# The root of the mean square by token: partition sums by ones and ScalarE's Sqrt in place of roots on diagonals

## The chip, the core and the metric

The kernel runs on one core of one Trainium2 chip. A core has TensorE (PE, matmuls; PEld is its loading of weights), VectorE (DVE), ScalarE (ACT), GpSimd (POOL) and the queue that issues DMAs (SP). The engines run beside one another and wait for each other by semaphores; each takes its own instructions in the order in which the program has them. PE writes its results into PSUM, from where DVE and ACT read them in this kernel. The metric is the device time of one execution in microseconds.

## The reference, cut to what matters

Eight sequences of 576 tokens go through windowed attention with 8 heads (four with a plain window of 32, four with a window of 128 of which every fourth token counts), then through a gated feed-forward layer whose input is normalised by token:

```python
scores = np.where(masks, scale * q @ k.T, -1e9)
attn = softmax(scores)
x = (attn @ v)                       # (4608 tokens, 512)
rms = np.sqrt(np.mean(x * x, axis=-1, keepdims=True) + 1e-06)
xn = x / rms * rms_g
g = xn @ w_gate                      # (512, 1536)
silu = g * (1.0 / (1.0 + np.exp(-g)))
val = xn @ w_val
return (silu * val @ w_out)          # (1536, 512)
```

The change is about the line with `rms`.

## The kernel before

The 4608 tokens are cut into 16 units of 288 (`U`). The activations lie with the 512 features on partitions, as four chunks of 128 (`c`), and the tokens along the free axis. A unit's feed-forward layer runs over 12 pieces `j` of 128 hidden features. For each j there are three steps: `gate` (12 matmuls for g), `val` (12 for v) and `proj` of the piece before (12 into the four accumulators `acc`), so 36 steps for a unit. From unit 1 on every operand is split into two float32r parts, a high one (a cast) and a low one (the difference), and a product takes three matmuls: high by high, high by low, low by high. Unit 0 works with whole float32 operands while the weights are still being loaded and decoded; unit 1 runs while they are being split.

The code writes the order out by hand. `now` counts steps; `later(dt, rank, fn)` puts work for the other engines into the step `now + dt`, and `flush`, ahead of each step's matmuls, issues what was put there, by rank. So a step's matmuls and what the other engines do with the results of the step before stand side by side. `plan` lays the attention of unit u (scores, transposes, outputs) over the 36 steps in which unit u-1 is multiplied; its dictionary `events` also holds two entries for the mean square of unit u:

- `"sum"` (L749) calls `rms_sum`, and `"apply"` (L750) calls `rms_apply`. For units from 2 on they come 3 and 5 steps behind the last attention output: in the step of v for j=9 and in that of g for j=10.

Where the mean square comes from: `square` (L423) squares each chunk of x on ACT and adds the four into one tile `xsq` (128 partitions by 288 tokens); the last addition is on DVE (L433). What is missing then is the sum over the 128 partitions and the root. Before the change:

- `rms_sum` (L526) has PE multiply `xsq`, in three blocks of 96 tokens, with a column of 1/512 (`inv`); the result `rps` has tokens on partitions, 96 by 3.
- `rms_root` (L534) adds 1e-6 on DVE (L536), raises to the power -0.5 on POOL (L537), and splits the result into two float32r parts on POOL (L542, L543).
- `spread`, a step later, lays both parts on diagonals: the high one by one DVE multiplication with the identity (L551), the low one by three ACT instructions (L555).
- `rms_apply` (L567) has PE multiply ones with the two diagonals, so that each of the 128 partitions holds the inverse root for all 288 tokens (`bps`, in PSUM). `normal(c)` (L585, DVE) multiplies a chunk by it and by the gain; `part(c)` splits it (L602 on ACT, L603 on DVE or POOL).

Around it each j has, outside PE: `tanh` of g on ACT (L661), one step behind the gate; `silu` on DVE (L666); `prod` with v on DVE (L679); the split of the result on ACT (L690) and POOL (L691), which `proj` needs two steps later. g and v have two PSUM banks that change places (`bank`): g of j+1 is written where v of j was, and v of j+1 where g of j was. The probabilities transposed by PE in a step go into the tail of such a bank, in a proj step into that of g of the same j (tile `t`). `split` casts keys and queries of the next unit (L330, L339 on ACT; L335 on POOL, L344 on DVE), and the softmax of the next unit takes L361 to L366 on DVE, L376 on ACT, L385 to L386 on DVE and L391 on POOL.

Unit 0 has its own way (`spread_first`, whole float32 tiles).

Of the kernel before, what the change touches and what calls it, by code (L numbers as in the profile page):

```python
# [9 lines left out]
F32 = mybir.dt.float32  # L10
# [10 lines left out]
P = 128  # L21
# [4 lines left out]
QB = 96  # L26
# [41 lines left out]
def attn_moe(ctx: ExitStack, tc: tile.TileContext, qk_in, v_in, w_gate, w_val, w_out, rms_g, outT):  # L68
# [14 lines left out]
    G.memset(one, 1.0)  # L83
    ones = cst.tile([P, P], F32R, name="ones")
    A.copy(out=ones, in_=one.to_broadcast([P, P]))
    inv = cst.tile([P, 2], F32, name="inv")
    G.memset(inv, 1.0 / DM)
    mhalf = cst.tile([QB, U // QB], F32, name="mhalf")
# [21 lines left out]
    def later(dt, rank, fn):  # L110
        put_off.setdefault(now[0] + dt, []).append((rank, fn))
# [411 lines left out]
    NB = U // QB  # L523
    rst = {}

    def rms_sum(u):  # L526
        r_ps = ps.tile([QB, NB, 2], F32, tag="o", name=f"rps_{u}")
        for i in range(NB):
            PE.matmul(r_ps[:, i, :], xsq[u][:, i * QB:(i + 1) * QB], inv, start=True, stop=True)
        later(1, 0.1, lambda: rms_root(u, r_ps))  # L530
        if u == 0:
            later(1, 6, spread_first)

    def rms_root(u, r_ps):  # L534
        r = sb.tile([QB, NB], F32, tag="rst", name=f"rst_{u}", bufs=2)
        V.tensor_scalar(out=r, in0=r_ps[:, :, 0], scalar1=1e-6, scalar2=None, op0=ALU.add)  # L536
        G.tensor_tensor(out=r, in0=r, in1=mhalf, op=ALU.pow)  # L537
        if u == 0:
            rst[u] = [r]
            return  # L540
        r_hi, r_lo = (sb.tile([QB, NB], F32R, tag=f"rst_{p}", name=f"rst_{p}_{u}", bufs=1) for p in ("hi", "lo"))
        G.tensor_copy(out=r_hi, in_=r)  # L542
        G.tensor_tensor(out=r_lo, in0=r, in1=r_hi, op=ALU.subtract)  # L543
        rst[u] = []

        def spread():
            for p in (r_hi, r_lo):
                d = sb.tile([QB, NB, QB], F32R, tag="tmp", name=f"rd_{u}_{len(rst[u])}", bufs=2)
                rst[u].append(d)
                if p is r_hi:  # L550
                    V.tensor_tensor(out=d, in0=ident[:QB, None, :QB].to_broadcast([QB, NB, QB]),  # L551
                                    in1=p[:, :, None].bitcast(F32).to_broadcast([QB, NB, QB]), op=ALU.mult)
                    continue
                for i in range(NB):
                    A.activation(out=d[:, i, :], in_=ident, func=AF.Copy, scale=p[:, i:i + 1].bitcast(F32))  # L555
        later(1, 0.1, spread)

    def spread_first():
        r, = rst[0]
# [7 lines left out]
    def rms_apply(u):  # L567
        ds = rst.pop(u)
        b_ps = ps.tile([P, U], F32, tag="o", name=f"bps_{u}")
        for k, d in enumerate(ds):  # L570
            PE.matmul(b_ps, (ones if u else ones32)[:QB, :], d.rearrange("p i q -> p (i q)"),
                      start=k == 0, stop=k == len(ds) - 1)
        xs[u] = {}
        if u == 0:
            root.append(sb.tile([P, U], F32, tag="tmp", name="root", bufs=2))
            later(1, 0.62, lambda: V.tensor_copy(out=root[0], in_=b_ps))

        def normal(c):
            x = xraw[u, c]
            if u == 0:  # L580
                xn = sb.tile([P, U], F32, tag="xhi", name=f"xn_{c}", bufs=4)
                V.tensor_tensor(out=xn, in0=x, in1=b_ps, op=ALU.mult)
                xs[u][c] = xn
                return
            V.scalar_tensor_tensor(out=x, in0=x, scalar=gs[:, c:c + 1], in1=b_ps,  # L585
                                   op0=ALU.mult, op1=ALU.mult)

        def part(c):
            x = xraw.pop((u, c))
            k = (u * NC + c) % 6  # L590
            if u > 1 and not spare:
                spare.append(cst.tile([P, 3, U], F32R, tag=f"slot{state['free']}", name="spare"))
            if k == 5 and u > 1:
                hi = spare[0][:, 2]
            else:
                pool, tag, bufs = (sb, "xhi", 4) if k < 4 else (late[0], ("xhi", "ot")[k - 4], 1)
                hi = pool.tile([P, U], F32R, tag=tag, name=f"xhi_{u}_{c}", bufs=bufs)
            if c < 2 and u % 2 == 0:
                lo = spare[0][:, c]
            else:  # L600
                lo = late[0].tile([P, U], F32R, tag=f"xlo{c // 2}", name=f"xlo_{u}_{c}", bufs=2)
            A.copy(out=hi, in_=x)  # L602
            (V if c % 2 else G).tensor_tensor(out=lo, in0=x, in1=hi, op=ALU.subtract)  # L603
            xs[u][c] = (hi, lo)

        for c in range(NC):
            later((1, 2, 2, 3)[c] if u else 1, 0.6 + (0.03 * (c > 1) if u == 0 else 0), lambda c=c: normal(c))
            if u:
                later((2, 3, 4, 5)[c], 0.6, lambda c=c: part(c))


    hs, acc, gv = {}, {}, {}
# [132 lines left out]
    def plan(u, base, q_at, t_at, o_at):  # L745
        for b, *ts in zip(bursts(u), q_at, t_at, o_at):
            for kind, t in zip("qto", ts):
                events.setdefault(base + t, {})[kind] = b
        events.setdefault(base + o_at[-1] + (4 if u == 1 else 3), {})["sum"] = u  # L749
        events.setdefault(base + o_at[-1] + (4, 7, 5)[min(u, 2)], {})["apply"] = u  # L750

    def attend(t_ps, **tags):
        e = events.pop(now[0], {})
# [132 lines left out]
```

## Time and profile before

| | |
|---|---|
| median of 3 runs | 1148.58 us (1146.93 to 1150.12) |
| the profiled execution | 1148.22 us |
| its span, from first to last instruction | 1146.4 us |
| granted TensorE clock, mean | 0.997 |
| read from HBM, written | 71.08 MB, 9.44 MB |

The span is what the profile covers; the 1.8 us between it and the execution's time lie around it. The profile names an instruction by its line in the kernel, its engine, and output and input. A timeline has the start in microseconds from the beginning of the span, the length, and in square brackets the idle time of the engine just before it with what ended it. Matmuls are pipelined: one that is said to last 0.29 us begins 0.13 us behind the one before it. In a view of groups the columns behind the count are the busy time in all, the mean of one in ns, and the idle time ahead of them. Short pieces of a timeline may overlap by some 0.1 us on one engine, since the next instruction starts before the last one is through.

### The profile page before, as it was taken

To read this page: it belongs to the slowest core of one execution; us is meant where nothing else is said; L and a number is where in the kernel's file an instruction comes from. 1 tells how busy PE (TensorE), PEld (TensorE's weight loads), DVE (VectorE), ACT (ScalarE), POOL (GpSimd) and SP (SyncE) were. 2 spreads that over 40 slices of the span, in tenths; PEclk is the share of its full clock that TensorE was granted. 3 is DMA by queue.
4 is the path that set the end of the run, shared out by engine and by line. 5 is a ranking of instruction groups with operands and counts; after the bars stand their busy time and mean duration, and the time that the engine had idled before them with its cause. 6 is when DMAs were issued, how large, how long until landed. Compare 5 with 4: busy or idle time off the path is not lost.

```text
span 1146.4 us, 25956 instructions
## 1 busy us (share of the span) xinstructions
PE 1120.8 (98%) x8357; PEld 1088.0 (95%) x8357; DVE 793.4 (69%) x2893; ACT 714.6 (62%) x2610; POOL 620.8 (54%) x1073
## 2 busy tenths in 40 slices
PE   8898888999999999999999999999999999999998
PEld 7676778999999999999999999999999999999998
DVE  7889865867767586776758677585866758586411
ACT  5686676766657576675757657576765757576311
POOL 8235576655546465564547556465655646565211
PEclk9999999999999999999999999999999999999999
DMA  9555211311212121121212213121221312120000
GB/s 246 168 202 205 89 48 38 93 50 50 83 38 82 40 84 52 52 89 33 79 41 83 58 41 94 34 86 41 71 63 45 95 27 87 41 79 15 2 21 21
DMA packets 61545, 82.19 MB, mean 72 GB/s; under 512 B 7298, under 2 KB 41090, under 8 KB 61410
## 3 DMA queue, kind: packets, MB, share of 16 engines
q1 hardware_dynamic: 61410, 80.54, 23.6%
q8 instruction: 67, 1.10, 0.4%
q14 instruction: 68, 0.56, 0.2%
HBM read 71.08 MB, written 9.44 MB: 70 GB/s over the span
## 4 chain that ended last, share of the span: by engine, by line
PE 85%; DVE 6%; ACT 4%; issue 2%; DMA 1%; POOL 1%; POOLq 0%; SPq 0%; DVEq 0%; ACTq 0%
PE acc L622 8%; PE g L622 8%; PE v L622 8%; PE acc L623 8%; PE g L624 8%; PE g L623 8%; PE acc L624 8%; PE v L623 8%; PE v L624 8%; PE s L489 3%; PE o L477 3%; PE o L478 1%; PE busy L739 1%; ACT t L376 1%; DVE lo L243 1%
## 5 line engine op out<-in xcount | busy, mean ns | idle before, releaser
L691 POOL TENSOR_TENSOR hlo<-th,hhi 128x288 fp32r<-128x288 f32 x180 | 145.2, 807 | 201.5 <-ACT hhi L690 153.7
L624 PE MATMUL acc<-hhi,lo 128*128 128x288 f32 x720 | 212.2, 295 | 0.0
L391 POOL TENSOR_SCALAR t<-t,sum 72x72 f32<-72x72 f32 (+3 forms) x414 | 154.0, 384 | 71.9 <-DVE sum L386 65.2
L624 PE MATMUL v<-xhi,lo 128*128 128x288 f32 x612 | 180.8, 295 | 0.0
L624 PE MATMUL g<-xhi,lo 128*128 128x288 f32 x612 | 180.6, 295 | 0.0
L376 ACT ACTIVATE t<-t,sum 96x128 f32<-96x128 f32 (+3 forms) x448 | 165.6, 375 | 11.7 <-DVE sum L366 11.0
L690 ACT CAST hhi<-th 128x288 fp32r<-128x288 f32 x180 | 78.1, 434 | 141.0 <-DVE th L679 138.8
L305 POOL TENSOR_TENSOR vlo<-vt,vhi 128x128 fp32r<-128x128 f32 x196 | 93.3, 476 | 109.3 <-ACT vhi L301 96.9
L421 DVE TENSOR_TENSOR xraw<-o,xraw 64x96 f32<-64x96 f32 (+1 forms) x392 | 106.8, 272 | 56.4 <-ACT xraw L411 50.4
L661 ACT ACTIVATE th<-g 128x288 f32<-128x288 f32 x180 | 73.9, 410 | 106.6 <-PE g L624 87.7
L624 PEld LDWEIGHTS acc<-hhi,lo 128*128 128x128 f32 x720 | 135.6, 188 | 0.0
L666 DVE SCALAR_TENSOR_TENSOR th<-th,g 128x288 f32<-128x288 f32 x180 | 80.4, 447 | 69.4 <-ACT th L661 69.4
L624 PEld LDWEIGHTS v<-xhi,lo 128*128 128x128 f32 x612 | 115.3, 188 | 0.0
L624 PEld LDWEIGHTS g<-xhi,lo 128*128 128x128 f32 x612 | 115.0, 188 | 0.0
L622 PE MATMUL g<-xhi,hi_g 128*128 128x288 f32 x357 | 110.7, 310 | 1.6 <-DVE sum L385 0.9
L335 POOL TENSOR_TENSOR ks<-qk,ks 128x288 fp32r<-128x288 f32 (+2 forms) x112 | 111.0, 1005 | 0.0
L622 PE MATMUL acc<-hhi,hi_o 128*128 128x288 f32 x360 | 110.8, 308 | 0.0
L411 ACT COPY xraw<-o 64x96 f32<-64x96 f32 (+1 forms) x392 | 101.5, 259 | 12.5 <-PE o L478 10.1
L679 DVE TENSOR_TENSOR th<-th,v 128x288 f32<-128x288 f32 x180 | 81.5, 453 | 38.1 <-PE v L624 30.0
L623 PE MATMUL acc<-hlo,hi_o 128*128 128x288 f32 x360 | 106.9, 297 | 0.0
L361 DVE TENSOR_TENSOR t<-s,mask 96x256 f32<-96x256 f32 (+3 forms) x196 | 71.5, 365 | 50.9 <-PE s L489 45.7
L623 PE MATMUL g<-xlo,hi_g 128*128 128x288 f32 x322 | 94.8, 294 | 0.0
(184 smaller groups left out, 3581.2 us busy)
## 6 DMA issues: line engine op xcount, KB each, us to landing
qk<-in_qk_dram SPq DMA_DIRECT2D x60, 288.0 KB, 2.8
vt<-in_v_dram SPq DMA_DIRECT2D x196, 64.0 KB, 1.9
qk<-in_qk_dram SPq DMA_DIRECT2D x30, 352.0 KB, 3.0
out_dram<-ot SPq DMA_DIRECT2D x64, 144.0 KB, 1.9
qk<-in_qk_dram SPq DMA_DIRECT2D x30, 304.0 KB, 2.8
raw<-in_w_gate_dram SPq DMA_DIRECT2D x12, 512.0 KB, 4.7
raw<-in_w_val_dram SPq DMA_DIRECT2D x12, 512.0 KB, 5.3
raw<-in_w_out_dram SPq DMA_DIRECT2D x12, 512.0 KB, 4.3
```

The source lines that it names most:

```text
L305: G.tensor_tensor(out=vl, in0=vs.pop(b), in1=vh, op=ALU.subtract)
L335: ek.tensor_tensor(out=ks[:, 1, :nkt], in0=kr, in1=ks[:, 0, :nkt], op=ALU.subtract)
L376: A.activation(out=t[:nq, a, :n], in_=t[:nq, a, :n], func=AF.Exp, scale=-1.0, bias=sm[:nq, a, 0:1], accum_out=sm[:nq, a, 1:2] if u else None)
L391: (V if u == 0 and (c, i) > (NC - 1, 0) else G).tensor_scalar(out=t[:nq, a, :n], in0=t[:nq, a, :n], scalar1=sm[:nq, a, 3:4], scalar2=1.0, ...
L411: A.copy(out=to[a * D:(a + 1) * D], in_=o[a * D:(a + 1) * D, (2 + a) * nq:(3 + a) * nq])
L421: V.tensor_tensor(out=to[rows], in0=o[rows, a * nq:(a + 1) * nq], in1=to[rows], op=ALU.add)
L622: PE.matmul(out, wh[:, cc, :], xh, start=start, stop=False)
L623: PE.matmul(out, wh[:, cc, :], xl, start=False, stop=False)
L624: PE.matmul(out, wl[:, cc, :], xh, start=False, stop=stop)
L666: V.scalar_tensor_tensor(out=t, in0=t, scalar=1.0, in1=g, op0=ALU.add, op1=ALU.mult)
L679: V.tensor_tensor(out=t, in0=t, in1=v_ps[:, :U], op=ALU.mult)
L691: G.tensor_tensor(out=lo, in0=t, in1=hi, op=ALU.subtract)
```

## The change

For the units from 1 on, the sum over partitions, the root and the spreading over partitions are done in another way:

- `rms_sum` no longer has PE do anything; it puts `rms_parts` into the next step. That splits `xsq` into two float32r parts: the high one by a cast on ACT, the low one by a subtraction on DVE.
- `rms_apply` has PE multiply a 128 by 128 matrix of ones with both parts. The result (`bps`) is, on every partition, the sum of squares of each token.
- One step later ACT takes the root, Sqrt(bps / 512 + 1e-6), out of PSUM into the tile `mean`; a step after that DVE takes the reciprocal in place. `normal(c)` reads `mean` instead of `bps`.
- The events move: for units from 2 on `"sum"` comes one step earlier (2 behind the last output instead of 3) and `"apply"` one earlier (4 instead of 5); for unit 1 likewise (3 instead of 4, 6 instead of 7). Counted from `apply`, `normal` and `part` come one step later, and so they stay in the same steps as before.

The diagonals, the power on POOL and the small matmuls remain for unit 0 alone.

```diff
--- before.py
+++ after.py
@@ -83,6 +83,8 @@
     G.memset(one, 1.0)
     ones = cst.tile([P, P], F32R, name="ones")
     A.copy(out=ones, in_=one.to_broadcast([P, P]))
+    eps = cst.tile([P, 1], F32, name="eps")
+    G.memset(eps, 1e-6)
     inv = cst.tile([P, 2], F32, name="inv")
     G.memset(inv, 1.0 / DM)
     mhalf = cst.tile([QB, U // QB], F32, name="mhalf")
@@ -523,37 +525,28 @@
     NB = U // QB
     rst = {}
 
+    def rms_parts(u):
+
+        parts = [sb.tile([P, U], F32R, tag="tmp", name=f"sq{p}_{u}", bufs=2) for p in ("hi", "lo")]
+        A.copy(out=parts[0], in_=xsq[u])
+        V.tensor_tensor(out=parts[1], in0=xsq[u], in1=parts[0], op=ALU.subtract)
+        rst[u] = parts
+
     def rms_sum(u):
+        if u:
+            later(1, 0.45, lambda: rms_parts(u))
+            return
         r_ps = ps.tile([QB, NB, 2], F32, tag="o", name=f"rps_{u}")
         for i in range(NB):
             PE.matmul(r_ps[:, i, :], xsq[u][:, i * QB:(i + 1) * QB], inv, start=True, stop=True)
         later(1, 0.1, lambda: rms_root(u, r_ps))
-        if u == 0:
-            later(1, 6, spread_first)
+        later(1, 6, spread_first)
 
     def rms_root(u, r_ps):
         r = sb.tile([QB, NB], F32, tag="rst", name=f"rst_{u}", bufs=2)
         V.tensor_scalar(out=r, in0=r_ps[:, :, 0], scalar1=1e-6, scalar2=None, op0=ALU.add)
         G.tensor_tensor(out=r, in0=r, in1=mhalf, op=ALU.pow)
-        if u == 0:
-            rst[u] = [r]
-            return
-        r_hi, r_lo = (sb.tile([QB, NB], F32R, tag=f"rst_{p}", name=f"rst_{p}_{u}", bufs=1) for p in ("hi", "lo"))
-        G.tensor_copy(out=r_hi, in_=r)
-        G.tensor_tensor(out=r_lo, in0=r, in1=r_hi, op=ALU.subtract)
-        rst[u] = []
-
-        def spread():
-            for p in (r_hi, r_lo):
-                d = sb.tile([QB, NB, QB], F32R, tag="tmp", name=f"rd_{u}_{len(rst[u])}", bufs=2)
-                rst[u].append(d)
-                if p is r_hi:
-                    V.tensor_tensor(out=d, in0=ident[:QB, None, :QB].to_broadcast([QB, NB, QB]),
-                                    in1=p[:, :, None].bitcast(F32).to_broadcast([QB, NB, QB]), op=ALU.mult)
-                    continue
-                for i in range(NB):
-                    A.activation(out=d[:, i, :], in_=ident, func=AF.Copy, scale=p[:, i:i + 1].bitcast(F32))
-        later(1, 0.1, spread)
+        rst[u] = [r]
 
     def spread_first():
         r, = rst[0]
@@ -568,9 +561,15 @@
         ds = rst.pop(u)
         b_ps = ps.tile([P, U], F32, tag="o", name=f"bps_{u}")
         for k, d in enumerate(ds):
-            PE.matmul(b_ps, (ones if u else ones32)[:QB, :], d.rearrange("p i q -> p (i q)"),
-                      start=k == 0, stop=k == len(ds) - 1)
+            if u:
+                PE.matmul(b_ps, ones, d, start=k == 0, stop=k == len(ds) - 1)
+            else:
+                PE.matmul(b_ps, ones32[:QB, :], d.rearrange("p i q -> p (i q)"), start=True, stop=True)
         xs[u] = {}
+        if u:
+            mean = sb.tile([P, U], F32, tag="tmp", name=f"mean_{u}", bufs=2)
+            later(1, 2.2, lambda: A.activation(out=mean, in_=b_ps, func=AF.Sqrt, scale=1.0 / DM, bias=eps))
+            later(2, -0.5, lambda: V.reciprocal(out=mean, in_=mean))
         if u == 0:
             root.append(sb.tile([P, U], F32, tag="tmp", name="root", bufs=2))
             later(1, 0.62, lambda: V.tensor_copy(out=root[0], in_=b_ps))
@@ -582,7 +581,7 @@
                 V.tensor_tensor(out=xn, in0=x, in1=b_ps, op=ALU.mult)
                 xs[u][c] = xn
                 return
-            V.scalar_tensor_tensor(out=x, in0=x, scalar=gs[:, c:c + 1], in1=b_ps,
+            V.scalar_tensor_tensor(out=x, in0=x, scalar=gs[:, c:c + 1], in1=mean,
                                    op0=ALU.mult, op1=ALU.mult)
 
         def part(c):
@@ -604,9 +603,9 @@
             xs[u][c] = (hi, lo)
 
         for c in range(NC):
-            later((1, 2, 2, 3)[c] if u else 1, 0.6 + (0.03 * (c > 1) if u == 0 else 0), lambda c=c: normal(c))
+            later((2, 3, 3, 4)[c] if u else 1, 0.6 + (0.03 * (c > 1) if u == 0 else 0), lambda c=c: normal(c))
             if u:
-                later((2, 3, 4, 5)[c], 0.6, lambda c=c: part(c))
+                later((3, 4, 5, 6)[c], 0.6, lambda c=c: part(c))
 
 
     hs, acc, gv = {}, {}, {}
@@ -746,8 +745,8 @@
         for b, *ts in zip(bursts(u), q_at, t_at, o_at):
             for kind, t in zip("qto", ts):
                 events.setdefault(base + t, {})[kind] = b
-        events.setdefault(base + o_at[-1] + (4 if u == 1 else 3), {})["sum"] = u
-        events.setdefault(base + o_at[-1] + (4, 7, 5)[min(u, 2)], {})["apply"] = u
+        events.setdefault(base + o_at[-1] + (3, 3, 2)[min(u, 2)], {})["sum"] = u
+        events.setdefault(base + o_at[-1] + (4, 6, 4)[min(u, 2)], {})["apply"] = u
 
     def attend(t_ps, **tags):
         e = events.pop(now[0], {})
```

What it moves on ACT, around tanh of j=9 and j=10 of unit 3, in which the mean square of unit 4 is formed (`th` and `g` carry unit and j, `ks`, `qs` and `t` unit 5, whose attention is under way, `hhi` is the high part of the product, `rd` and `mean` belong to unit 4). Before:

```order
L661 ACTIVATE th_3_9_4531<-g_3_9_4515 128x288
L330 CAST ks_5_2_4539<-qk_5_2_4170 128x320
L690 CAST hhi_3_9_4566<-th_3_9_4531 128x288
L376 ACTIVATE t_5_0_0_4534,sum0_86<-t_5_0_0_4534,sum0_86 96x128 x2
L330 CAST ks_5_3_4572<-qk_5_3_4204 128x320
L339 CAST qs_5_2_4574<-qk_5_2_4170 128x288
L555 ACTIVATE rd_4_1_4594<-ident_64,rst_lo_4_4563 96x96 x3
L339 CAST qs_5_3_4605<-qk_5_3_4204 128x288
L661 ACTIVATE th_3_10_4628<-g_3_10_4608 128x288
```

After:

```order
L660 ACTIVATE th_3_9_4503<-g_3_9_4487 128x288
L531 CAST sqhi_4_4506<-sq_4_0_3842 128x288
L332 CAST ks_5_2_4515<-qk_5_2_4142 128x320
L689 CAST hhi_3_9_4531<-th_3_9_4503 128x288
L378 ACTIVATE t_5_0_0_4510,sum0_88<-t_5_0_0_4510,sum0_88 96x128 x2
L332 CAST ks_5_3_4537<-qk_5_3_4176 128x320
L341 CAST qs_5_2_4539<-qk_5_2_4142 128x288
L571 ACT_TABLE_LOAD
L571 ACTIVATE mean_4_4560<-bps_4_4557,eps_73 128x288
L341 CAST qs_5_3_4569<-qk_5_3_4176 128x288
L660 ACT_TABLE_LOAD
L660 ACTIVATE th_3_10_4590<-g_3_10_4572 128x288
```

The three instructions on the diagonal give way to a table load and Sqrt, a cast of the sum of squares comes in behind tanh of j=9, and ahead of tanh of j=10 stands a second table load: the program loads one set of functions for Sqrt and then the one for tanh and the exponential again. The first load waits for the two bps matmuls, the second for g of j=10.

On DVE, from the last addition of squares to the mask addition behind the product of j=9, and then from the reciprocal of the softmax's sums to the product of j=10 (`xraw` is a chunk of unit 4 that `normal` multiplies). Before, the first piece:

```order
L433 TENSOR_TENSOR sq_4_0_3870<-sq_4_0_3870,sq_4_3_4513 128x288
L361 TENSOR_TENSOR t_5_0_0_4534<-s_5_0_0_4528,mask_77 96x256
L366 ISA t_5_0_0_4534,sum0_86<-s_5_0_0_4528,t_5_0_0_4534 96x128
L366 ISA sum0_86 96x1
L366 ISA t_5_0_0_4534,sum0_86<-s_5_0_0_4528,t_5_0_0_4534 96x128
L366 ISA sum0_86 96x1
L666 SCALAR_TENSOR_TENSOR th_3_9_4531<-th_3_9_4531,g_3_9_4515 128x288
L679 TENSOR_TENSOR th_3_9_4531<-th_3_9_4531,v_3_9_4541 128x288
L536 TENSOR_SCALAR rst_4_4559<-rps_4_4554 96x3
L551 TENSOR_TENSOR rd_4_0_4592<-ident_64,rst_hi_4_4562 96x288
L361 TENSOR_TENSOR t_5_0_1_4598<-s_5_0_1_4589,mask_77 96x256
```

After, the first piece and then the second:

```order
L435 TENSOR_TENSOR sq_4_0_3842<-sq_4_0_3842,sq_4_3_4485 128x288
L532 TENSOR_TENSOR sqlo_4_4507<-sq_4_0_3842,sqhi_4_4506 128x288
L363 TENSOR_TENSOR t_5_0_0_4510<-s_5_0_0_4500,mask_79 96x256
L368 ISA t_5_0_0_4510,sum0_88<-s_5_0_0_4500,t_5_0_0_4510 96x128
L368 ISA sum0_88 96x1
L368 ISA t_5_0_0_4510,sum0_88<-s_5_0_0_4500,t_5_0_0_4510 96x128
L368 ISA sum0_88 96x1
L665 SCALAR_TENSOR_TENSOR th_3_9_4503<-th_3_9_4503,g_3_9_4487 128x288
L678 TENSOR_TENSOR th_3_9_4503<-th_3_9_4503,v_3_9_4517 128x288
L363 TENSOR_TENSOR t_5_0_1_4561<-s_5_0_1_4554,mask_79 96x256
```

```order
L388 RECIPROCAL sum0_88<-sum0_88 96x2
L572 RECIPROCAL mean_4_4560<-mean_4_4560 128x288
L584 SCALAR_TENSOR_TENSOR xraw_4_0_3656<-xraw_4_0_3656,gs_87,mean_4_4560 128x288
L665 SCALAR_TENSOR_TENSOR th_3_10_4590<-th_3_10_4590,g_3_10_4572 128x288
L346 TENSOR_TENSOR qs_5_3_4569<-qk_5_3_4176,qs_5_3_4569 64x288
L678 TENSOR_TENSOR th_3_10_4590<-th_3_10_4590,v_3_10_4599 128x288
```

The low part `sqlo` now stands behind the addition of squares and ahead of the mask addition, where it waits for ACT's cast; the small instruction on `rps` and the diagonal `rd` are gone. In the second piece the reciprocal of `mean` stands ahead of the first normalisation; silu and the product of j=10 follow behind it, in the order that they had before.

On PE the pair of bps matmuls goes from behind g of j=10 to ahead of it, behind the scores of that step. Before it stood between g and v:

```order
L623 MATMUL g_3_10_4608<-xlo_3_3_3656,hi28_o8_1966 128x288
L624 MATMUL g_3_10_4608<-xhi_3_3_3655,lo_14_1967 128x288
L571 MATMUL bps_4_4621<-rd_4_0_4592,ones_71 128x288
L571 MATMUL bps_4_4621<-rd_4_1_4594,ones_71 128x288
L622 MATMUL v_3_10_4637<-xhi_3_0_3560,hi28_o8_1966 128x288
```

After:

```order
L491 MATMUL s_5_0_1_4554<-ks_5_0_4071,qs_5_0_4108 96x256
L491 MATMUL s_5_0_1_4554<-ks_5_1_4106,qs_5_1_4144 96x256
L565 MATMUL bps_4_4557<-sqhi_4_4506,ones_71 128x288
L565 MATMUL bps_4_4557<-sqlo_4_4507,ones_71 128x288
L621 MATMUL g_3_10_4572<-xhi_3_0_3532,hi28_o8_1958 128x288
```

The rps matmuls, which stood between v of j=9 and the projection of j=8, are gone.

## The prediction

> **What bounds the kernel now.** I read the head of the page first, then the busy times by stretch, then the timelines of PE, VectorE (DVE) and ScalarE (ACT) around one place where the change acts.
>
> ```profile
> span 1146.4 us, 25956 instructions
> PE 1120.8 (98%) x8357; PEld 1088.0 (95%) x8357; DVE 793.4 (69%) x2893; ACT 714.6 (62%) x2610; POOL 620.8 (54%) x1073
> PE 85%; DVE 6%; ACT 4%; issue 2%; DMA 1%; POOL 1%; POOLq 0%; SPq 0%; DVEq 0%; ACTq 0%
> ```
>
> A PE busy for 98% need not be a PE at its limit, so the stretches come next (start and end, length, then busy time of PE, PEld, DVE, ACT, POOL, the granted clock, the DMA share and GB/s):
>
> ```profile
> 110.00:183.00 73.00, 61.53 (x386) 54.39 (x384) 56.67 (x181) 48.25 (x166) 47.99 (x69) 0.98 0.22 68
> 183.00:1075.00 892.00, 890.84 (x6946) 887.31 (x6947) 628.03 (x2400) 573.77 (x2169) 506.59 (x910) 1.00 0.20 59
> ```
>
> From 183 to 1075 us PE has no gaps (890.84 of 892, at clock 1.00): what PE no longer does there is saved, and what makes PE wait there is lost. The stretch 110 to 183 has 11.5 us of gaps, and there other engines set the pace. The units 2 to 14 have their normalisation in the full stretch, unit 1 in the looser one, unit 15 at its end. I follow unit 4, while unit 3 is multiplied. PE (start, length):
>
> ```profile
> 332.20 0.30 PE L624 MATMUL v<-xhi,lo 128*128 128x288 f32 x1
> 332.34 0.59 PE L529 MATMUL rps<-inv,sq 128*96 128x2 f32 x6
> 332.79 0.38 PE L622 MATMUL acc<-hhi,hi_o 128*128 128x288 f32 x1
> ...
> 336.16 0.30 PE L624 MATMUL g<-xhi,lo 128*128 128x288 f32 x1
> 336.29 0.43 PE L571 MATMUL bps<-rd,ones 96*128 96x288 f32 x2
> 336.56 0.30 PE L622 MATMUL v<-xhi,hi_o 128*128 128x288 f32 x1
> ...
> 339.95 0.33 PE L463 MATMUL t<-ident,t 96*128 96x96 f32 x2
> 340.06 0.38 PE L622 MATMUL g<-xhi,hi_g 128*128 128x288 f32 x1
> ```
>
> The g that begins at 340.06 (j=11) writes the PSUM bank in which v of j=10 lies, so it needs that v to have been read by the product in DVE (L679); the transposes at 339.95 need the bank of g of j=10, which tanh (ACT) and silu (DVE, L666) read. These are the two releases to watch. DVE at this place:
>
> ```profile
> 329.81 0.46 DVE L433 TENSOR_TENSOR sq<-sq,sq 128x288 f32<-128x288 f32 x1 [0.51 <-ACT sq L427]
> 330.95 0.42 DVE L361 TENSOR_TENSOR t<-s,mask 96x256 f32<-96x256 f32 x1 [0.68 <-PE s L489]
> ...
> 331.84 0.45 DVE L666 SCALAR_TENSOR_TENSOR th<-th,g 128x288 f32<-128x288 f32 x1
> 332.54 0.46 DVE L679 TENSOR_TENSOR th<-th,v 128x288 f32<-128x288 f32 x1 [0.26 <-PE v L624]
> ...
> 337.94 0.49 DVE L585 SCALAR_TENSOR_TENSOR xraw<-xraw,gs,bps 128x288 f32<-128x288 f32 x1
> 338.35 0.44 DVE L666 SCALAR_TENSOR_TENSOR th<-th,g 128x288 f32<-128x288 f32 x1
> 338.82 0.46 DVE L344 TENSOR_TENSOR qs<-qk,qs 64x288 fp32r<-64x288 f32 x1
> 339.31 0.46 DVE L679 TENSOR_TENSOR th<-th,v 128x288 f32<-128x288 f32 x1
> ```
>
> The product of j=10 ends at 339.77, and PE takes the bank at 340.06: **0.3 us of room**, no more. ACT:
>
> ```profile
> 330.78 0.41 ACT L661 ACTIVATE th<-g 128x288 f32<-128x288 f32 x1 [0.99 <-PE g L624]
> ...
> 333.03 0.43 ACT L690 CAST hhi<-th 128x288 fp32r<-128x288 f32 x1 [1.49 <-DVE th L679]
> 333.37 0.40 ACT L376 ACTIVATE t<-t,sum 96x128 f32<-96x128 f32 x1
> ...
> 334.15 0.44 ACT L330 CAST ks<-qk 128x320 fp32r<-128x320 f32 x1
> 334.50 0.43 ACT L339 CAST qs<-qk 128x288 fp32r<-128x288 f32 x1
> 334.89 0.91 ACT L555 ACTIVATE rd<-ident,rst_lo 96x96 fp32r<-96x96 f32 x3
> 335.71 0.42 ACT L339 CAST qs<-qk 128x288 fp32r<-128x288 f32 x1
> 336.55 0.41 ACT L661 ACTIVATE th<-g 128x288 f32<-128x288 f32 x1 [0.42 <-POOL ks L335]
> ```
>
> **What the change removes.** The rps matmuls take PE from 332.34 to 332.79, 0.45 us, and the matmul behind them lasts 0.38 instead of 0.29, which I count as 0.09 more: 0.54 us for a unit. The two bps matmuls have 128 rows in place of 96 and the same 288 columns, so they are left at 0.27 us (336.29 to 336.56). DVE loses its small row out of PSUM and the diagonal, ACT 0.9 us of diagonals (334.89), POOL its power and two small ones. No DMA moves. By PE alone the 13 units of the full stretch give 13 x 0.54 = 7.0 us, all 15 give 8.1.
>
> **What it adds on ACT: two table loads in a unit.** The changed program has a load ahead of Sqrt and one ahead of the next tanh. The trace has one such load, and what came behind it:
>
> ```profile
> 0.72 1.28 ACT L85 ACT_TABLE_LOAD   x1 [0.72 <-PEq L874]
> 2.02 0.30 ACT L85 CAST ones<-one 128x128 fp32r<-128x128 f32 x1
> ```
>
> I take 1.28 us for each: the next instruction began 0.02 us after it. [...] Sqrt itself and the operations beside it, from rows of the same shape:
>
> ```profile
> L427 ACT ACTIVATE sq<-xraw 128x288 f32<-128x288 f32 x64 | 27.9, 437 | 5.9 <-DVE xraw L421 4.9 <-DVE xraw L408 0.9
> L603 DVE TENSOR_TENSOR xlo<-xraw,xhi 128x288 fp32r<-128x288 f32 x16 | 11.2, 700 | 3.6 <-ACT xhi L602 3.6
> L679 DVE TENSOR_TENSOR th<-th,v 128x288 f32<-128x288 f32 x180 | 81.5, 453 | 38.1 <-PE v L624 30.0 <-PE v L463 5.5
> L386 DVE RECIPROCAL sum<-sum 96x2 f32<-96x2 f32 x96 | 15.8, 165 | 3.3
> L385 DVE TENSOR_REDUCE sum<-sum 96x2 f32<-96x4 f32 x96 | 14.6, 153 | 1.9
> ```
>
> Sqrt 0.44 us; the cast to the high part 0.43 (L690's row); the low part on DVE 0.45 to 0.70, of which I take 0.45 and keep 0.25 for the range.
>
> **What it adds on DVE: a reciprocal of 128x288.** No row shows one of that width. The lower end is that of any DVE operation of this width, 0.45 us (L679). The upper end comes from the two small rows: the reduction reads 4 elements in 153 ns, the reciprocal 2 in 165. At about 1 ns an element the reduction has 149 ns without its elements; if the 16 ns above that are the price of two elements, one costs 8 ns, and 288 cost 2.3 us: 2.45 us in all. If the 16 ns are a fixed delay, the lower end holds. I take **2.45**, since the only row of this operation is the longer of the two although it handles fewer elements. [...]
>
> **The chain, in the times of unit 4.** ACT makes the high part behind tanh of j=9: some 331.1 to 331.5. DVE waits for it with the low part, 331.5 to 331.95; behind it in DVE's queue stand the mask addition (which began at 330.95, now 1.0 later), silu and the product of j=9. Silu comes at 332.85, the product at 333.3 to 333.75, and so ACT's cast hhi at 333.8 instead of 333.03. From hhi to the place of the diagonals ACT needs 334.89 - 333.03 = 1.86 us: 335.7. There stands the first load, whose wait for bps is over (PE has written it by 334.6). Load to 337.0, Sqrt to 337.45, qs to 337.8, second load to 339.1, tanh of j=10 to 339.5 (today 336.96). On DVE the reciprocal waits for Sqrt: 337.45 to 339.9; then the normalisation, 0.41 us to the next start, silu at 340.3, and the product 0.96 later as today (338.35 to 339.31): 341.27 to 341.73. PE, without its rps, would want the bank at 340.06 - 0.54 = 339.52 and gets it at 341.75: **2.2 us of stall**, less 0.54 saved, is 1.7 us lost in a unit. Behind that PE and DVE are as far apart as today, so I let nothing be won back or lost again.
>
> Sum: 13 units x 1.7 = 22 us. Unit 15 has no next unit's softmax and casts in ACT's queue, and unit 1 lies where the weights are still being decoded and PE waits anyway; I leave both at nothing, 3 us either way. The profiled execution took 1148.22 us for its span of 1146.4, so it would take 1170; the median of the runs, 1148.58, is 0.4 higher: **1171 us**.
>
> **Rivals.**
> 1. *The reciprocal is as cheap as other operations* (0.45). Then tanh comes last, at 339.5; silu follows at once, the product ends at 340.92, the stall is 1.4 and the net loss 0.86 us: 13 x 0.86 = 11, 1160 us. For it: 16 ns may be a fixed delay.
> [...]
> 3. *It ends faster*: ACT is idle for 1.49 us ahead of hhi and 0.99 ahead of tanh, and if the loads run in such idle time and the reciprocal is cheap, Sqrt ends at 336.15, tanh near 336.9 and the product by 338.4, ahead of PE's 339.52. Nothing stalls, and the 8.1 us of rps are won: 1140 us. It decides where the product ends before 340.06; with the cheap reciprocal and both loads in line it ends 0.86 later than that. Against it: the first load stands behind hhi and waits for bps, the second waits for g of j=10, so neither can be moved into the idle time ahead of them.
> 4. *About no change*: stall and saving cancel, 0.54 us against 0.54.
>
> **How the numbers follow.** Forecast 0.56 (its own range 1163 to 1185, with the 0.25 us of the low part in 13 units, 3.3 us, the 3 us of units 1 and 15, and half a us a unit for what the walk leaves out), cheap reciprocal 0.20, dearer switches 0.09, faster 0.11, no change 0.04. The range 1147 to 1185 leaves out the dearer and the faster case, 0.20. About 0.3% can be told from no change here: faster 0.11, within it 0.04, slower 0.85.
>
> **What would show it.** In the profile after: 30 more table loads of about 1.28 us with no idle time behind them; the row of the reciprocal near 2.4 us; in each of the units 2 to 14 one gap of PE of some 2.2 us ahead of the transposes and g of j=11, released by silu or the product; tanh of j=10 about 3 us behind the end of g; elsewhere a PE as full as before. PE gaps elsewhere, a gap that starts at bps, or a gap that the reciprocal's length doesn't explain would make the chain above wrong; no gap at all would leave rival 3.

## The result and the profile after

The changed kernel takes **1175.89 us** (median of 4 runs, 1174.48 to 1176.28) against 1148.74 us of the kernel before on the same chip (4 runs): 1.0238 times as long, 95% interval 1.0224 to 1.0253. The forecast was 1171 us, in a range of 1147 to 1185. The profiled execution took 1176.28 us, for a span of 1174.2; before it was 1148.22 and 1146.4. The span has grown by 27.8 us.

The head of the page after:

```profile
span 1174.2 us, 25717 instructions
PE 1126.0 (96%) x8267; PEld 1085.2 (92%) x8267; DVE 812.7 (69%) x2893; ACT 752.0 (64%) x2625; POOL 601.4 (51%) x1029
```

PE has 90 instructions fewer and yet a longer busy time, and its share of the span has fallen from 98% to 96%. The view of PE's waits from 183 to 1100 us (what PE waited for, us in total, times, longest) names two:

```profile
PE t L465 <- DVE th L665: 13.6, 13, 1.1
PE g L621 <- DVE th L678: 6.9, 13, 0.5
```

Thirteen of each, one pair in each of the units 2 to 14, released by silu (L665) and by the product (L678). Lines have moved up by one: L660 is tanh, L665 silu, L678 the product, L689 the cast hhi. What the change added, in the view of groups (busy us, mean ns of one, idle time ahead of them and its releaser):

```profile
L572 DVE RECIPROCAL mean<-mean 128x288 f32<-128x288 f32 x15 | 29.3, 1953 | 13.7 <-ACT mean L571 13.7
L571 ACT ACT_TABLE_LOAD x15 | 19.2, 1283 | 1.0 <-PE bps L565 0.7
L660 ACT ACT_TABLE_LOAD x15 | 19.2, 1283 | 0.3
L571 ACT ACTIVATE mean<-bps,eps 128x288 f32<-128x288 f32 x15 | 7.5, 502 | 0.7 <-PE bps L565 0.6
L532 DVE TENSOR_TENSOR sqlo<-sq,sqhi 128x288 fp32r<-128x288 f32 x15 | 6.9, 459 | 17.6 <-ACT sqhi L531 17.6
```

Thirty loads of 1283 ns as forecast; the reciprocal takes 1953 ns, not 2450. The last line also shows a wait: ahead of the low part DVE stands idle for ACT's cast sqhi, 17.6 us over the 15 units. Unit 4 in the timeline of ACT (start, length, idle time ahead in brackets):

```profile
339.40 0.43 ACT L689 CAST hhi<-th 128x288 fp32r<-128x288 f32 x1 [2.08 <-DVE th L678]
...
340.87 0.43 ACT L341 CAST qs<-qk 128x288 fp32r<-128x288 f32 x1
341.31 1.28 ACT L571 ACT_TABLE_LOAD   x1
342.61 0.50 ACT L571 ACTIVATE mean<-bps,eps 128x288 f32<-128x288 f32 x1
343.01 0.42 ACT L341 CAST qs<-qk 128x288 fp32r<-128x288 f32 x1
343.45 1.28 ACT L660 ACT_TABLE_LOAD   x1
344.74 0.41 ACT L660 ACTIVATE th<-g 128x288 f32<-128x288 f32 x1
```

of DVE:

```profile
343.14 1.95 DVE L572 RECIPROCAL mean<-mean 128x288 f32<-128x288 f32 x1 [0.82 <-ACT mean L571]
345.13 0.52 DVE L584 SCALAR_TENSOR_TENSOR xraw<-xraw,gs,mean 128x288 f32<-128x288 f32 x1
345.57 0.45 DVE L665 SCALAR_TENSOR_TENSOR th<-th,g 128x288 f32<-128x288 f32 x1
346.04 0.45 DVE L346 TENSOR_TENSOR qs<-qk,qs 64x288 fp32r<-64x288 f32 x1
346.53 0.45 DVE L678 TENSOR_TENSOR th<-th,v 128x288 f32<-128x288 f32 x1
```

and of PE:

```profile
339.61 0.29 PE L565 MATMUL bps<-sqhi,ones 128*128 128x288 f32 x1
...
346.16 0.36 PE L465 MATMUL t<-ident,t 96*128 96x96 f32 x2 [1.13 <-DVE th L665]
347.04 0.40 PE L621 MATMUL g<-xhi,hi_g 128*128 128x288 f32 x1 [0.52 <-DVE th L678]
```

ACT goes from the first load to tanh without a gap, DVE from the reciprocal to the product, and PE takes the bank 0.06 us behind the end of the product (346.53 + 0.45): it is the forecast chain, at the forecast place.

What a unit costs is read from the first bps matmul of unit 2 and that of unit 15, 13 units on. The groups of PE's bps rows from 183 us on, first of before, then of after (the last of the 28 rows of before is the second of its pair, 0.1 us behind the first):

```profile
L571 PE MATMUL bps<-rd,ones x28: 290/297/300, 201.8 to 1075.4; 96*128 96x288 f32 x28
```

```profile
L565 PE MATMUL bps<-sqhi,ones x14: 294/295/299, 200.0 to 1100.7; 128*128 128x288 f32 x14
```

Before, (1075.3 - 201.8) / 13 = 67.19 us for a unit; after, (1100.7 - 200.0) / 13 = 69.28. So 13 x 2.09 = 27.2 of the 27.8 us come from these thirteen units, and units 1 and 15 with all the rest give 0.6. The forecast for a unit was 1.7; the experiments show what makes it 2.09.

### The profile page after: what moved, and what is told of

Its sections match the earlier page's. It is cut to its first block, busy times and chain, and to the rows that moved or that the text cites. A ratio compares the mean times of both kernels' runs of the same rounds, so it can differ in the third digit from the quotient of the medians.

```text
span 1174.2 us, 25717 instructions
## 1 busy us (share of the span) xinstructions
PE 1126.0 (96%) x8267; PEld 1085.2 (92%) x8267; DVE 812.7 (69%) x2893; ACT 752.0 (64%) x2625; POOL 601.4 (51%) x1029
## 4 chain that ended last, share of the span: by engine, by line
PE 69%; DVE 14%; ACT 10%; issue 4%; DMA 2%; POOL 1%; SPq 0%; POOLq 0%; DVEq 0%; ACTq 0%
PE g L621 7%; PE g L623 7%; PE g L622 7%; PE v L621 7%; PE acc L621 7%; PE acc L622 6%; PE acc L623 6%; PE v L623 6%; PE v L622 6%; DVE mean L572 3%; PE o L479 2%; PE s L491 2%; ACT t L378 2%; DVE th L678 2%; DVE t L368 1%
## 5 line engine op out<-in xcount | busy, mean ns | idle before, releaser
L689 ACT CAST hhi<-th 128x288 fp32r<-128x288 f32 x180 | 78.0, 433 | 138.2 <-DVE th L678 136.0
L660 ACT ACTIVATE th<-g 128x288 f32<-128x288 f32 x180 | 73.8, 410 | 99.6 <-PE g L623 83.4
L665 DVE SCALAR_TENSOR_TENSOR th<-th,g 128x288 f32<-128x288 f32 x180 | 80.4, 447 | 66.8 <-ACT th L660 66.8
L678 DVE TENSOR_TENSOR th<-th,v 128x288 f32<-128x288 f32 x180 | 81.6, 453 | 36.3 <-PE v L623 24.4
```

The source lines that it names most:

```text
L665: V.scalar_tensor_tensor(out=t, in0=t, scalar=1.0, in1=g, op0=ALU.add, op1=ALU.mult)
L678: V.tensor_tensor(out=t, in0=t, in1=v_ps[:, :U], op=ALU.mult)
```

## The experiments

Each kernel is the changed one with the edit shown. The ratios are to the kernel before, on the same chip. "A unit" is again the distance from bps to bps, from rows like the two above.

**Loads and reciprocal, one at a time and together.** Three kernels show what each costs; for what they leave out of the computation see their expectations.

```diff
-  A.activation(out=mean, in_=b_ps, func=AF.Sqrt, ...)
+  A.activation(out=mean, in_=b_ps, func=AF.Tanh, ...)      # e1, e3
-  V.reciprocal(out=mean, in_=mean)
+  V.tensor_scalar(out=mean, in0=mean, scalar1=1.0, scalar2=None, op0=ALU.mult)   # e2, e3
```

> The changed kernel with Tanh in the place of Sqrt (same shape, scale and bias, so the inverse root is not what is computed), and so without the two table loads of a unit. Chain theory: ACT reaches this instruction 1.28 us earlier, 1.7 us behind the bps matmuls; DVE is free for the reciprocal at 2.7, so it ends at 4.66 instead of 5.49, the product of j=10 at 6.55 instead of 7.38; the stall of PE falls from 2.07 to 1.24 us in each of the units 2 to 14, net of the 0.54 saved 0.70 x 13 = 9 us: 1158 us, and no stretches of half clock behind 130 us. Rival, loads alone make the loss: about 1141 us. Rival, the reciprocal alone makes it: no change from 1176 us.

> The changed kernel with a multiplication by 1.0 in the place of the reciprocal (so x is multiplied by the root). Chain theory: the product now waits for tanh behind the second load, which ends 5.55 us behind bps; silu 5.6 to 6.0, product to 7.0, stall 1.69 instead of 2.07, net 1.15 x 13 = 15 us: 1164 us, with fewer stretches of half clock than four. Rival, the reciprocal alone makes the loss: about 1141 us. Rival, loads alone: no change from 1176 us.

> Both edits at once: Tanh for Sqrt and a multiplication for the reciprocal. Chain theory: the product of j=10 ends 5.0 us behind bps, ahead of the 5.36 at which PE wants the bank; no stall, and what is left is the saving of the rps matmuls in the full stretch, 13 x 0.54 = 7 us or 8 with all units: 1141 us, PE without gaps from 183 us on, no stretch of half clock there. Rival, the new sums cost PE as much as the old ones: 1149 us.

Measured: without loads 1159.57 us (1.0097, 1.0080 to 1.0114); with the short operation 1167.2 (1.0161, 1.0146 to 1.0176); with both edits 1141.76 (0.9938, 0.9923 to 0.9953). PE's waits without loads:

```profile
PE g L621 <- DVE th L678: 6.9, 13, 0.5
PE t L465 <- DVE th L665: 1.4, 7, 0.2
```

and with the short operation:

```profile
PE t L465 <- DVE th L665: 8.7, 13, 0.8
PE g L621 <- DVE th L678: 6.9, 13, 0.5
```

With both edits PE has no wait for silu or the product at all, and a window on the full stretch (start and end, length, busy time of PE, PEld, DVE, ACT, POOL, clock, DMA share, GB/s) has PE full:

```profile
183.00:1070.00 887.00, 885.78 (x6884) 881.72 (x6883) 623.98 (x2401) 569.86 (x2154) 493.95 (x867) 1.00 0.20 59
```

Its PE from the same bps on, for unit 4, and the whole row of bps:

```profile
332.50 0.29 PE L565 MATMUL bps<-sqhi,ones 128*128 128x288 f32 x1
...
337.88 0.38 PE L621 MATMUL g<-xhi,hi_g 128*128 128x288 f32 x1
```

```profile
L565 PE MATMUL bps<-sqhi,ones x14: 294/295/299, 198.6 to 1065.6; 128*128 128x288 f32 x14
```

Two things follow. A unit takes (1065.6 - 198.6) / 13 = 66.69 us, 0.50 less than before: that is the saving of rps, forecast at 0.54. And from bps to g of j=11 an unstalled PE needs 337.88 - 332.50 = 5.38 us; in the changed kernel it is 347.04 - 339.61 = 7.43. **The stall in unit 4 is 2.05 us** (forecast 2.2). It is so in seven of the thirteen units; in the other six, which alternate with them, the same distance is 7.26 us and the stall 1.88. The mean is 1.97. The two waits of unit 4 show 1.65 of its stall; the rest is in the modelled ends of the matmuls ahead of them. With either of the two in place every unit still stalls (67.19 became 68.01 us a unit with the reciprocal alone, 68.61 with the loads alone); with neither, none does.

**The low part on POOL.**

```diff
-  V.tensor_tensor(out=parts[1], in0=xsq[u], in1=parts[0], op=ALU.subtract)
+  G.tensor_tensor(out=parts[1], in0=xsq[u], in1=parts[0], op=ALU.subtract)
```

> The changed kernel with the low part of the sum of squares on POOL instead of DVE; all else, loads and reciprocal too, stays. Chain theory: DVE no longer waits for ACT's cast, the product of j=9 and ACT's cast hhi come 0.9 us earlier, and so does all that follows in ACT's queue: the stall falls from 2.07 to about 1.2 us, net 0.65 x 13 = 8 us: 1157 us, no stretch of half clock behind 183 us. Rival, the place of the low part has nothing to do with it, only loads and reciprocal: no change from 1176 us.

Measured: 1159.24 us (1.0093, 1.0078 to 1.0108). An operation of 459 ns on DVE and its wait for ACT's cast, ahead of everything that the product of j=9 waits for, cost 16.65 us over the kernel, 1.28 for each of the 13 units. In unit 4 the cast hhi now begins 1.13 us ahead of bps, not 0.21, and the loads with it; bps to g of j=11 takes 6.51 us, not 7.43. So 0.9 us of the 1.28 are the delay that the prediction put at 0.77 (hhi at 333.8 instead of 333.03). The next part turns to the rest.

**The clock.** Stall less saving is 1.97 - 0.50 = 1.47 us, and a unit has grown by 2.09. The windows from bps to bps of the changed kernel show where more goes (the clock stands third from the end):

```profile
200.00:270.70 70.70, 68.86 (x519) 68.07 (x519) 50.35 (x183) 46.51 (x167) 38.01 (x66) 0.98 0.21 60
270.70:339.60 68.90, 67.23 (x520) 66.16 (x519) 48.54 (x183) 45.46 (x167) 36.00 (x66) 1.00 0.20 59
...
477.10:547.40 70.30, 68.65 (x520) 68.08 (x519) 49.42 (x183) 46.62 (x167) 38.21 (x66) 0.98 0.21 60
...
485.12:488.53 3.41, 3.41 (x16) 3.41 (x16) 2.95 (x13) 2.04 (x8) 2.94 (x4) 0.50 0.35 106
...
486.00:487.00 1.00, 1.00 (x6) 1.00 (x6) 0.97 (x8) 0.88 (x4) 1.00 (x3) 0.50 0.43 169
...
489.00:490.00 1.00, 1.00 (x10) 1.00 (x10) 0.48 (x3) 0.44 (x2) 0.59 (x1) 1.00 0.00 0
```

Four of the thirteen units have a clock of 0.98 and take 70.3 to 70.7 us, the other nine 68.5 to 69.4 (mean 68.8) at 1.00. The four are among the units with the longer stall; the other three of these take 69.1 us in the mean, 1.3 less than the four. In each of the four the clock is 0.50 for 3.4 us just behind the stall, while PE is busy again: in the last two rows, 2 and 5 us behind the stall that ended at 484.6, PE begins 6 matmuls in a microsecond and then 10. The kernels without loads and with the low part on POOL have none behind 183 us, nor has the one with the short operation. A kernel with more reciprocals and one with a slightly longer stall test it:

```diff
-  later(2, -0.5, lambda: V.reciprocal(out=mean, in_=mean))
+  later(2, -0.5, lambda: [V.reciprocal(out=mean, in_=mean) for _ in range(3)])   # e6
+  later(2, -0.5, lambda: (V.reciprocal(out=mean, in_=mean),                      # e7
+        V.tensor_scalar(out=mean, in0=mean, scalar1=1.0, scalar2=None, op0=ALU.mult)))
```

> The changed kernel with the reciprocal taken three times in a row (the same value up to rounding). Chain theory without the clock: each of the 13 units stalls 3.9 us more, 5.97 in all; units 1 and 15 also lose some 4 each: 1176 + 51 + 8 = 1235 us, less the four stretches of half clock of the changed kernel (6.8) if the clock has nothing to do with the stalls. Clock theory: a stall of 6 us covers at least one whole interval of 3.413 us, so a stretch of half clock follows in every unit, 13 or more instead of four, each costing up to 1.7 us: 1235 to 1255 us. Rival, the half clock comes by chance or by load elsewhere: no more stretches than four or five.

> The changed kernel with a multiplication by 1.0 behind the reciprocal, 0.31 us. Chain theory: stall of 2.4 us instead of 2.07, 13 x 0.31 = 4 us: 1180 us if the stretches of half clock stay at four. Clock theory: the share of an interval that PE idles grows, so more units than 4 of 13 are followed by half clock, perhaps 6 to 9: 1183 to 1189 us.

Measured, in one run each: 1253.88 us with three reciprocals, 1184.22 with the extra multiplication. With three, every one of the 13 units has a clock below 1.00 (0.95, one of them 0.98), and PE's longest wait is 5.1 us:

```profile
PE t L465 <- DVE th L665: 65.3, 13, 5.1
...
L565 PE MATMUL bps<-sqhi,ones x14: 294/295/299, 202.9 to 1172.5; 128*128 128x288 f32 x14
```

A unit takes 969.6 / 13 = 74.58 us, 5.30 more than with one. Two more reciprocals are 3.91 us; the 1.39 beyond them fit the clock, which is low in every unit instead of in four, but no run takes them apart. At 0.95 over a unit it is low for twice as long, and it falls while PE still waits, so that a part of the time costs nothing: in the unit from 351.5 us on the clock is 0.50 from some 360.4 to 367.3 us, and PE's wait ends at 362.0. With the extra multiplication six of the 13 units are at 0.98. They take 70.5 us in the mean, the other seven 69.2. So a stretch of 3.4 us costs 1.3 us in this kernel as in the changed one, by the means of the units; an estimate of the most is 1.7, half its length, since the clock is 0.50 in it. By these two the four of the changed kernel cost **5 to 7 us**. The expectation of the three reciprocals lets the fall follow whole intervals without PE; stalls of 2.05 us, shorter than a stretch, brought it on in 4 of 13 units too.

Why in these four? By the clock rows of the trace their stretches are 3.413 us long and begin at 208.64, 485.12, 761.60 and 901.54 us, which is 81, 81 and 41 times 3.413 us apart: they lie on a fixed grid of intervals. The next two rows are intervals of that grid. The clock falls behind the first, which holds the stall of unit 6, and not behind the second, which holds a part of that of unit 4:

```profile
481.71:485.12 3.41, 1.76 (x13) 1.37 (x12) 3.31 (x7) 2.30 (x8) 0.00 (x0) 1.00 0.06 24
345.17:348.58 3.41, 1.90 (x13) 1.74 (x14) 3.31 (x10) 2.11 (x9) 0.98 (x2) 1.00 0.27 67
```

The stall of unit 6 ends at 484.58 and lies wholly in its interval. That of unit 4 is as long, but begins 0.3 us ahead of the border at 345.17, and so PE is busy for 0.14 us more of the interval. In the changed kernel the clock falls behind each interval from 183 us on in which PE is busy for 1.75 to 1.77 us, and behind none with 1.90 or more. With the extra multiplication it falls behind 1.41 to 1.59 us and not behind 1.82 or more; with the short operation no interval has less than 2.1. So here it depended on how a stall of some 2 us lay on the grid. The border value is rough, since the ends of matmuls are modelled: with three reciprocals three intervals with 1.6 to 1.7 us are not followed by half clock.

The clock does not explain all. The stalls less the saving make 13 x 1.47 = 19.1 us and the four stretches, by the estimate above, 5 to 7; of the 27.2 us some 1 to 3 are left. A part of them shows when PE's starts are laid beside those of the kernel with neither load nor reciprocal: in unit 5, at full clock, PE is 1.88 us later at g of j=11, and 0.4 us later still at the scores and v that follow. What holds it there was not tested.

**Can it be had without the stall?** Four kernels look for an order with the same result. The first has the low part on POOL, a tiny Sqrt on ACT right behind the cast sqhi that brings the first load forward, bps and the root one step earlier, the reciprocal behind the product of j=9, and the first normalisation one step later, behind the product of j=10; the other three stay in their steps:

```diff
+  if u > 1: A.activation(out=dum, in_=one, func=AF.Sqrt)
...
-  later(1, 2.2, lambda: A.activation(... func=AF.Sqrt ...))
-  later(2, -0.5, lambda: V.reciprocal(out=mean, in_=mean))
+  later(1, 0.4 if u > 1 else 2.2, lambda: A.activation(... func=AF.Sqrt ...))
+  later(1 if u > 1 else 2, 0.6 if u > 1 else -0.5, lambda: V.reciprocal(...))
-  later((2, 3, 3, 4)[c] if u else 1, ..., lambda c=c: normal(c))
+  later((4, 4, 4, 5)[c] if u > 1 else ..., lambda c=c: normal(c))     # rank 0.6
...
-  ... + (4, 6, 4)[min(u, 2)], {})["apply"] = u
+  ... + (4, 6, 3)[min(u, 2)], {})["apply"] = u
```

> A version meant to beat both, with the reference's result: the low part on POOL; for units from 2 on bps one step earlier, behind v of j=9; a tiny Sqrt of a constant right behind the cast sqhi, so that the first table load falls into ACT's idle time ahead of hhi; Sqrt ahead of hhi and the second load behind it, ahead of the exponential; the reciprocal behind the product of j=9 on DVE; the first normalisation behind the product of j=10. Chain theory: Sqrt ends about 1.6 us ahead of where the three diagonals ended, tanh of j=10 starts some 0.8 us later than before the change and the product of j=10 ends within 0.1 us of where PE wants the bank: stall of 0 to 0.4 us, 1141 to 1146 us, no half clock behind 183 us. Rival, two loads and a reciprocal cost PE 1 us or more wherever they stand, since ACT and DVE have no room for them: 1155 us or more.

Measured: 1159.01 us (1.0096, 1.0079 to 1.0112), a miss. The old waits are gone and there is a new one. DVE, and PE behind it, in unit 4:

```profile
340.64 1.92 DVE L587 SCALAR_TENSOR_TENSOR xraw<-xraw,gs,mean 128x288 f32<-128x288 f32 x3
342.48 0.41 DVE L364 TENSOR_TENSOR t<-s,mask 96x256 f32<-96x256 f32 x1
...
343.58 0.45 PE L492 MATMUL s<-ks,qs 128*96 128x256 f32 x2 [0.95 <-DVE sum L388]
```

Three normalisations stand ahead of the mask addition, which reads the bank of the scores that PE wants for the next ones. So the next kernel puts them behind it (steps 4, 5, 5, 6 with rank 0.75, their split at 5, 6, 6, 7):

> The kernel of the experiment before (low part on POOL, a tiny Sqrt that brings the first load forward, root and reciprocal a step earlier), with one thing put right: the mask addition of the next scores, the two operations that read the bank of the scores, and the reduction now stand ahead of all but the first of the four normalisations on DVE, not behind three of them. The result is the reference's. If the 0.95 us that PE waited for the scores' bank in each unit is only the 1.92 us of normalisations that stood ahead (chain theory), the bank is free about 1.5 us before PE wants it, PE has no wait from 183 us on, and the removed rps matmuls show: 1159.0 - 13 x 0.95 = 1147 at most, and 1141 to 1143 if, as without loads and reciprocal, nothing else waits. If the root by ACT, with its loads and the reciprocal, crowds DVE and ACT so that any order makes something late (rival), PE waits again in each unit at another place, and the time stays at 1150 or more.

Measured: 1169.2 us (1.0185, 1.0171 to 1.0199), worse. The wait for the scores' bank is gone; now silu of j=11 comes late behind the normalisations, with it the product and the split `pt` of the transposed probabilities, and PE waits for that at g of the next unit's first piece:

```profile
PE g L624 <- DVE pt L451: 14.1, 13, 1.4
```

The third spreads them: the first into a gap of DVE behind the reciprocal, the second as in the first of these kernels, the third behind the mask addition (steps 2, 4, 4, 5; ranks 0.72, 0.6, 0.75, 0.6):

> As the two kernels before it, but the four normalisations are spread on DVE: the first into the 0.43 us in which DVE waits for ACT's cast behind the reciprocal, the second behind the product of j=10, the third behind the mask addition that reads the scores' bank, the fourth where it was in the first of the two (behind the three, ahead of the next mask addition). The result is the reference's. Chain theory: the mask addition comes about 1.4 us earlier than with three normalisations ahead of it (1.92 us, less one of 0.5), which is more than the 0.95 us that PE waited there; silu of j=11 is no later than in that kernel, in which PE had no wait for it; so PE has no wait from 183 us on, and the time is 1159.0 - 13 x 0.95 = 1147 to 1141 us. Rival (DVE and ACT too full in the steps of the normalisation for any order): PE waits 0.5 us or more in each unit at a third place, 1148 or more.

Measured in 11 runs: 1150.4 us, against 1148.43 in 14 runs of before: 1.0014, 1.0005 to 1.0023. It is the best of them and as fast as the kernel before within 0.3%, not faster. PE's waits from 183 to 1070 us:

```profile
PE v L624 <- DVE pt L451: 2.5, 13, 0.2
PE o L480 <- DVE xraw L424: 1.6, 6, 0.3
```

A unit takes 67.40 us, 0.71 more than with neither load nor reciprocal. The waits are put down to DVE, which has no gap in unit 4 from the reciprocal's start at 335.57 to 346.64. The fourth kernel takes one low part of x from DVE to POOL and puts the third normalisation behind `pt`:

> The kernel before with two more moves in units 2 to 15: the third normalisation behind the product of the softmax's transpose (pt, for which PE waited 0.16 us in each unit), and the low part of the second chunk of x (0.45 us or more) from DVE, which had no idle time for the 11 us behind the reciprocal, to POOL. The result is the reference's. In the kernel before PE took 0.71 us a unit more than in the kernel with neither loads nor reciprocal (67.40 against 66.69 from bps to bps). If DVE's full stretch behind the reciprocal is what is left (chain theory), about 0.5 us of it goes and the waits of 0.16 and 0.26 us with it: 13 x 0.35 to 13 x 0.7 = 5 to 9 us, 1141 to 1146 us, below both kernels. If it is something else, such as PE's order or ACT (rival), it stays at 1149 to 1151; if POOL is what becomes late (its casts of the next keys stand behind the added operation), PE waits for POOL and it is above 1151.

Measured: 1154.9 us (1.0054, 1.0041 to 1.0068), a miss again: the last two normalisations, one behind the other, now take 1.73 us in unit 4 instead of 0.94 as two do in the changed kernel, while POOL works beside them, and PE waits for 7.7 us in all between 183 and 1070 us, against 5.9 in the kernel before it, most of it here:

```profile
PE o L480 <- DVE xraw L424: 3.2, 7, 0.5
PE g L624 <- DVE pt L451: 2.6, 7, 1.3
```

Why two DVE operations last longer beside this POOL work was not measured by itself and stays open, as does whether some other order gets below the kernel before.

## Why the prediction held, and where it was off

**Direction and mechanism** were right. The steps of the chain, each against the moment at which an unstalled PE wants the bank (forecast 339.52; measured bps + 5.38 = 344.99):

| | forecast, us | measured, us |
|---|---|---|
| hhi of j=9 starts | -5.7 | -5.59 |
| first load starts | -3.8 | -3.68 |
| Sqrt ends | -2.07 | -1.88 |
| tanh of j=10 ends | -0.02 | +0.16 |
| reciprocal ends | +0.38 | +0.10 |
| silu starts | +0.78 | +0.58 |
| product ends | +2.21 | +1.99 |
| g of j=11 starts | +2.23 | +2.05 |

- *Removal of rps*, 0.54 us a unit: 0.50, shown by the kernel with neither load nor reciprocal.
- *Loads*, 1.28 us with nothing behind: the length is right 30 times, and there is no idle time behind 28 of them (in unit 1 the next instruction comes 0.6 us later). In unit 4 the load begins 0.01 us behind the cast ahead of it, and Sqrt 0.02 behind the load. Sqrt 0.44: 0.50. The low part 0.45: 0.46.
- *Reciprocal*, 2.45 us: **mis-sized**, 1.95. The two small rows gave 8 ns an element; by the new row against the small one it is (1953 - 165) / 286 = 6.25. The 1 ns an element that the forecast has for the reduction is what the rows of other operations give: (453 - 153) / (288 - 4) = 1.06, from the product and the reduction. The choice of the upper end was right: the other end, 0.45, was far off. What makes the 6.25 ns, no run takes apart.
- *Stall*, 2.2 us, net 1.66 a unit and 22 us in all: 2.05 in unit 4 and 1.97 in the mean, net 1.47, 19 us. The shorter reciprocal gave 0.5 back, and ACT, 0.1 to 0.2 later than walked, took a part of it.
- *Behind the stall nothing is lost again*: **this step failed.** In 4 of 13 units PE's clock fell to 0.50 for 3.4 us behind the stall, an estimated 5 to 7 us in all. That is most of the difference between the sum of the prediction, with its terms corrected (19 us), and the measured 27.2; some 1 to 3 us come with the small delays behind the stall. The total was so near to the forecast, 1175.9 against 1171, partly by luck: the stall was put too high by 3 us and the rest left out.
- *Units 1 and 15* at 0 within 3 us: 0.6 with all that lies outside the thirteen.

**The rivals.** *A cheap reciprocal* did not come, and its price was off too: where it was put in by the short operation, the kernel took 1167, not 1160. Tanh comes last there, as the rival said, but 0.2 us later than walked; the stall of unit 4 is 1.68 us, not 1.4, and a unit costs 1.42 us more than before the change, not 0.86. *Dearer switches* (0.09): no run shows a switch that costs more than its load's row of 1283 ns; in unit 4 the first load begins 0.01 us behind the cast ahead of it, the second 0.02 behind the cast ahead of it, and the next instructions 0.02 and 0.01 us behind the loads. *Faster with hidden loads*: not in this order; even with the loads moved to where ACT has room, 1150.4 is the best that was found. *No change*: stall and saving cancel only in that kernel, within 0.3%.

## What to carry to other kernels

A shorter path for the engine that bounds the kernel is worth what the others let through: here 0.5 us a unit on PE was bought with 5 us on ACT and DVE (two loads, Sqrt and the reciprocal) just ahead of a bank with 0.3 us of room. Walk the chain to each bank's release with the durations of like rows; the walk came within 0.3 us at every step. Where two engines are late side by side, as ACT and DVE here, taking the delay from one alone won less than its length: without 2.57 us of loads a unit became 1.27 us shorter (69.28 to 68.01), with the short operation in place of the reciprocal of 1.95 us 0.67 (to 68.61). Where PE was full, price a new stall above its length: in 4 of 13 units here the clock fell to 0.50 for 3.4 us behind it.

## What was not expected of the hardware

Half clock for 3.4 us, also behind stalls that are themselves shorter: in 4 of 13 units at 2.05 us, in 6 of 13 with 0.3 us more, in 13 of 13 at about 6 us (for some 6.9 us in the unit from 351.5 us on), in none of 13 with 1.1 us (no loads) or 1.7 (short operation). Where it fell on a busy PE, a stretch cost 1.3 us by the means of the units; an estimate of the most is 1.7, half its length. At stalls of some 2 us it depended on where the stall lay on a grid of 3.413 us: the clock fell where one interval took in the whole stall or nearly so. And a reciprocal of 128x288 takes 1953 ns on DVE, four times as long as a multiplication of the same shape (453 ns).
